# Seven block products instead of eight in the second feed-forward product of a top-k attention and ELU kernel

## The chip, the core and the metric

The kernel runs on one core of one Trainium2 chip. The metric is device time in microseconds. Before the change the median of three runs was 1619.19 us (1617.57 to 1620.54).

The engines are named as the profile names them: PE is the matrix engine (PEld its weight loads), DVE the vector engine, ACT the scalar engine, POOL the GpSimd engine, SP the engine that issues most transfers. SBUF is the on-chip memory, PSUM the memory that PE writes its products to; a bank of it holds 512 float32 values for each of 128 partitions.

## The reference

Inputs are q, k and v of 8 batches, 8 heads, 576 rows and 64 columns, a first weight matrix of 512 x 2048 and a second of 2048 x 512. Attention keeps the 32 highest scores of a row. Its result, 4608 tokens of 512 values, passes through a feed-forward layer with an ELU.

```python
scores = scale * np.matmul(q, k.transpose(0, 1, 3, 2))
kth = np.partition(scores, -top_k, axis=-1)[..., -top_k:-top_k + 1]
scores = np.where(scores >= kth, scores, -1000000000.0)
attn = np.exp(scores - np.max(scores, axis=-1, keepdims=True))
attn = attn / (np.sum(attn, axis=-1, keepdims=True) + 1e-09)
x = np.matmul(attn, v)            # heads side by side: 4608 x 512
h = x @ w_in                      # 4608 x 2048
g = np.where(h > 0.0, h, np.exp(np.minimum(h, 0.0)) - 1.0)
out = g @ w_out                   # 4608 x 512
```

Everything on PE is float32. One matmul of the source leaves two records of each kind in the trace, two weight loads and two matmuls.

## The kernel before

**Steps.** Attention is cut into 144 steps, 18 a batch. A step is one tile of 128 query rows with one pair of heads, or for the 64 rows that are left over in each batch one step for two pairs of heads. The main loop (line 711) writes, for step n, the instructions of several steps into the engines' queues, in an order fixed by hand (`manual_schedule`): the score products of step n + 2 on PE and their copy to SBUF on ACT (`scores`, lines 332 and 340), the search for the 32 highest of step n on DVE (`select`: 8 MAX8 and 6 MATCH_REPLACE8, lines 374 to 386), the masks of step n - 1 on ACT (`mask`, lines 406 and 407), its normalisation on POOL (`distance`, line 416, and `normalise`, lines 426 to 433), and for step n - 2 the transposes on PE and their copy on ACT (`turn`, lines 452 and 453). Once a group of tiles is turned, `attend` (line 479) multiplies it with v, and `finish` copies the result into `xT` (line 506). Each engine works through its own queue in order.

**Blocks.** The feed-forward layer works on blocks of one or two tiles of 128 tokens. The first two batches make five blocks of one tile (numbers 0 to 4) and two of two tiles; each later pair of batches makes four blocks of two tiles and one of one. That is 14 blocks of two tiles and 8 of one. When a block's attention is done, `ffn_pieces` adds its work to the list `ffn`, in pieces. A hidden piece (`hidden`) computes 128 of the 2048 hidden values for all tokens of the block: 4 matmuls whose moving operand has 256 columns for two tiles or 128 for one; then come the two halves of the ELU on ACT (lines 564 to 573) and their sum, the gate, on POOL (line 524) or DVE (line 526), which `close_gates` writes later. The result lies turned in `blk.gT`, as two halves of 8 chunks. A second-product piece (`project`) is a quarter of one tile's sum: 4 of 16 matmuls of 512 columns into one bank. The fourth piece of a tile copies the bank out (line 591) and stores it from SP's queue (line 594).

**Placing the pieces.** `feed` is called four times a step: after the first part of the search, after `mask(prev, 0)` and its part, after `turn` and `mask(prev, 1)` and their part, and after `normalise`. `normalise` so stands between the third and the fourth feed. A hidden piece of a two-tile block costs 1.85 units there, a second-product piece 3.55 (`PROJECT`). From the times at which blocks become ready, in steps, and from the work ahead of them (`due`), `feed` takes a pace in units a step and takes pieces from the list when half a piece's cost has come together.

**Buffers that the change touches.** `etpool` (2), `xpool` for `xT` of one-tile blocks (3), `opool` for the result (1), and the pools that `hook` opens once the weights have been decoded and the loading buffers are given up: `late["f"]` (two `n` buffers of 128 x 512), `late["g"]` (two halves of `gT`), `late["x"]` (two `xT`), `late["in"]`. `ps_f` has two banks for hidden and second products together.

Of the kernel before, what the change touches and what calls it, by code (L numbers as in the profile page):

```python
# [9 lines left out]
ALU = mybir.AluOpType  # L10
FP32 = mybir.dt.float32
# [9 lines left out]
HIDDEN = {1: 1.1, 2: 1.85}  # L21
PROJECT = 3.55
# [60 lines left out]
def kernel(  # L83
# [9 lines left out]
    nc = tc.nc  # L93
    P = nc.NUM_PARTITIONS
    B, H, S, D = q.shape
    dm, dff = moe_w_in.shape[0], moe_w_in.shape[1] // 2
# [5 lines left out]
    NC = dm // P  # L102
    NF = dff // P
    NG = NF // 2
    T = 2 * P
    KEYS, QUERIES = R, R + S
    Q = 32
# [5 lines left out]
    def pool(name, bufs, **kw):  # L113
        return ctx.enter_context(tc.tile_pool(name=name, bufs=bufs, **kw))
# [2 lines left out]
    kvpool = pool("kv", 5)  # L117
    scpool = pool("sc", 5)
    wkpool = pool("wk", 1)
    etpool = pool("et", 2)  # L120
    small = pool("small", 4)
    xpool = pool("x", 3)
    opool = pool("o", 1)
    ps_sc = pool("ps_sc", 1, space=PSUM)
    ps_t = pool("ps_t", 2, space=PSUM)
    ps_f = pool("ps_f", 2, space=PSUM)
    wide = [ps_sc.tile([P, 2, JP], FP32, tag=f"s{i}", name="scps") for i in range(2)]
    late = {}
    raws = ExitStack()
    early = raws.enter_context(tc.tile_pool(name="early", bufs=1))  # L130
    earlyf = raws.enter_context(tc.tile_pool(name="earlyf", bufs=2))
    ldpool = raws.enter_context(tc.tile_pool(name="ld", bufs=2))
# [7 lines left out]
    w_out = const.tile([P, NF, dm], FP32, tag="w_out", name="w_out")  # L140
# [59 lines left out]
    def hook():  # L200

        if not decode:
            return
        decode.pop(0)()
        if not decode:
            raws.close()
            late["f"] = ctx.enter_context(tc.tile_pool(name="f", bufs=2))
            late["g"] = ctx.enter_context(tc.tile_pool(name="g", bufs=2))
            late["x"] = ctx.enter_context(tc.tile_pool(name="xt", bufs=2))
            late["in"] = ctx.enter_context(tc.tile_pool(name="in", bufs=2))  # L210

    def decode_piece(i):
        if i + 3 < 2 * NF:
# [285 lines left out]

    def finish(blk, parts, at, cols, src):  # L500
        if blk.xT is None:
            if blk.slots == 1:
                blk.xT = xpool.tile([P, NC, P], FP32, tag="xT", name="xT")
            else:
                blk.xT = late["x"].tile([P, NC, T], FP32, tag="xT", name="xT")
        nc.scalar.copy(blk.xT[:, at, cols], src)
        blk.left -= parts
        if blk.left == 0:
            ffn.extend(ffn_pieces(blk))

    gates = []
    place = [0]

    def close_gates(keep=0, upto=None):

        while gates:
            put, group, dst, n, apart = gates[0]
            if put > place[0] - keep if upto is None else group > upto:  # L520
                return
            gates.pop(0)
            if apart:
                nc.gpsimd.tensor_tensor(dst, n, dst, ALU.add)  # L524
                continue
            nc.vector.scalar_tensor_tensor(
                out=dst, in0=n, scalar=-1.0, in1=dst, op0=ALU.add, op1=ALU.add
            )

    def ffn_pieces(blk):  # L530
        n_tok = blk.slots * P
        bank = dm // n_tok
        unit = max(2, bank)

        def hidden(f):
            if f == 0 and blk.number == 0:
                g = early.tile([P, NF, P], FP32, tag="g", name="gT")
                blk.gT = [g[:, 0:NG], g[:, NG:NF]]
            elif f % NG == 0 and blk.number > 0:
                g = late["g"].tile([P, NG, T], FP32, tag="g", name="gT")  # L540
                blk.gT.append(g[:])
            if f % unit == 0:
                if len(gates) > 1:
                    close_gates(upto=gates[0][1])
                if blk.number == 0:
                    n = earlyf.tile([P, 4 * P], FP32, tag="n", name="n")
                else:
                    n = late["f"].tile([P, 2 * T], FP32, tag="n", name="n")
                blk.n = n[:, 0 : unit * n_tok].rearrange("p (f t) -> p f t", f=unit)
            if f % bank == 0:  # L550
                ps = ps_f.tile([P, dm], FP32, tag="f", name="hps")
                blk.h = ps[:, 0 : bank * n_tok].rearrange("p (f t) -> p f t", f=bank)
            for i in range(NC):
                nc.tensor.matmul(  # L554
                    blk.h[:, f % bank, :],
                    w_in[:, i, f * P : (f + 1) * P],
                    blk.xT[:, i, 0:n_tok],
                    start=(i == 0),
                    stop=(i == NC - 1),
                )  # L560
            g, end = blk.gT[f // NG], f % NG + 1
            if end % bank == 0:
                n0 = f % unit + 1 - bank
                nc.scalar.activation(
                    blk.n[:, n0 : n0 + bank, :], blk.h, AF.Relu, scale=-1.0
                )
                nc.scalar.activation(g[:, end - bank : end, 0:n_tok], blk.h, AF.Relu)
            if end % unit == 0:
                nc.scalar.activation(blk.n, blk.n, AF.Exp, scale=-1.0)
                dst = g[:, end - unit : end, 0:n_tok]  # L570
                apart = place[0] > 4 * (tight + 3) and blk is not blocks[-1]
                if apart:
                    nc.scalar.activation(blk.n, blk.n, AF.Copy, bias=-1.0)  # L573
                gates.append((place[0], (blk.number, f + 1 - unit), dst, blk.n, apart))

        def project(s, part):
            close_gates(upto=(blk.number, (part + 1) * NF // 4 - 1))
            if part == 0:
                blk.o = ps_f.tile([P, dm], FP32, tag="f", name="ops")
            step = NF // 4  # L580
            for f in range(part * step, (part + 1) * step):
                nc.tensor.matmul(  # L582
                    blk.o[:],
                    blk.gT[f // NG][:, f % NG, s * P : (s + 1) * P],
                    w_out[:, f, :],
                    start=(f == 0),
                    stop=(f == NF - 1),
                )
            if part == 3:
                o = opool.tile([P, dm], FP32, tag="osb", name="osb")  # L590
                nc.scalar.copy(o[:], blk.o[:])
                for t in blk.tiles[s]:
                    p0 = t.cols.start - s * P
                    nc.sync.dma_start(out[t.rows, :], o[p0 : p0 + t.ql, :])

        part = HIDDEN[blk.slots]
        behind = 2 * NF if blk.number else 0
        return [
            (part, max(behind, NC * (f // 4 + 1)), lambda f=f: hidden(f))
            for f in range(NF)  # L600
        ] + [
            (PROJECT, max(behind, NF + (part + 1) * NF // 4),
             lambda s=s, part=part: project(s, part))
            for s in range(blk.slots)
            for part in range(4)
        ]

    ffn = []
    steps, first, due = [], {}, []
    blocks, tight = [], 2 * NHP  # L610
    for b in range(B):
        if b % 2 == 0:
# [5 lines left out]
            for part in division:  # L618
                blk = Block(len(blocks), len(part))
# [4 lines left out]
        for qt in range(J + 1):  # L624
# [8 lines left out]
            t = Tile(b, qt, rows, blk, slice(c0, c0 + n))  # L633
# [6 lines left out]
        for qts in order:  # L640
# [3 lines left out]
            for qt in qts:  # L644
                n = len(steps)
                tiles[qt].block.ready = n + 1.0 if n <= tight else n + 2.5
    NS = len(steps)
    total = 0.0
    for blk in sorted(blocks, key=lambda x: x.ready):
        due.append((blk.ready, total))  # L650
        total += NF * HIDDEN[blk.slots] + 4 * blk.slots * PROJECT

    todo = {}

# [3 lines left out]
    for b in range(1, B):  # L658
        f = first[b]
# [10 lines left out]
    def feed(n, share):  # L670

        place[0] += 1
        close_gates(2 if n < tight - 1 or n > tight + 1 else 6)
        fed["at"] = max(fed["at"], n)
        ahead = [(w - fed["sum"]) / (x - fed["at"]) for x, w in due if x > fed["at"]]
        if ahead:
            fed["over"] += max(0.0, share * min(ahead))
        fed["at"] += share
        while ffn and decoded[0] >= ffn[0][1] and 0.5 * ffn[0][0] <= fed["over"]:
            cost, _, piece = ffn.pop(0)  # L680
            fed["over"] -= cost
            fed["sum"] += cost
            piece()
# [118 lines left out]
```

## Time and profile before

| what | value |
|---|---|
| median of the runs | 1619.19 us |
| the profiled execution, its time | 1617.99 us |
| its span from first to last instruction | 1616.2 us |
| mean granted clock of PE | 0.974 |
| L554, hidden product: 2816 records | busy 541.8 us |
| L582, second product: 1152 records of 512 columns | busy 525.2 us |
| L386, MAX8 on DVE: 816 records | busy 654.2 us |
| L433, normalise on POOL: 288 records | busy 214.1 us |
| idle time of PE's transposes (L452) behind POOL's L433 | 32.9 us |

A row of a group reads: line, engine, operation, what is written and read, shapes, count, then busy time and mean duration in ns, then the idle time of the engine just before them and what ended it. A row of a stretch reads: the stretch, its length and PE's busy time, then PEld, DVE, ACT and POOL with counts, then the granted clock, the share of DMA and GB/s. A row of the waits names who waited for whom, the total, how often, and the longest. A row of the chain of waits, in order of time, has start, length and what ran; so has a row of the timeline, with the idle time before it in brackets. Busy time of PE is modelled and hides short gaps; the granted clock was below 1 only in the first 320 us.

### The profile page before, as it was taken

The page shows a single profiled execution, that of the slowest core. Times are in us where ns is not written, and L with a number is a line of the kernel's source. Part 1 is how long each engine was busy: PE and PEld are TensorE (multiplying, and loading weights), DVE is VectorE, ACT ScalarE, POOL GpSimd, SP SyncE. Part 2 cuts the span into 40 slices and gives each one's busy share as a digit, 9 for nine tenths or more (in the row PEclk, how much of TensorE's full clock was granted, in tenths as well). Part 3 has the DMA queues.
Part 4 walks back from the last instruction along what each step waited for, and adds up shares of the span by engine and source line. Part 5 has one row for each costly group of instructions (what it writes and reads, how often), then busy time and mean ns, then how long its engine had stood idle before and what let it go on. Part 6 is the DMA issues. An engine that isn't in the chain of part 4 may idle for free.

```text
span 1616.2 us, 25917 instructions
## 1 busy us (share of the span) xinstructions
PE 1572.3 (97%) x8660; PEld 1049.6 (65%) x8660; DVE 1451.6 (90%) x2981; ACT 1189.1 (74%) x2400; POOL 693.5 (43%) x1410
## 2 busy tenths in 40 slices
PE   5889999999999999999999999999999999999999
PEld 3565777666675757567475757577566666666764
DVE  6988999999999999999999599999999879999500
ACT  6988787778686868578686868777767776767831
POOL 3775444345353534345353444444434443533500
PEclk8579999999999999999999999999999999999999
DMA  7441220012100211002100121002200101000000
GB/s 220 157 136 27 51 41 23 8 22 45 43 1 14 43 33 28 14 16 50 38 8 7 23 51 37 8 8 44 52 15 7 22 16 36 1 14 7 1 13 14
DMA packets 188037, 56.21 MB, mean 35 GB/s; under 512 B 178176, under 2 KB 179200, under 8 KB 187904
## 3 DMA queue, kind: packets, MB, share of 16 engines
q1 hardware_dynamic: 186704, 54.26, 14.2%
q8 instruction: 69, 1.13, 0.3%
q14 instruction: 64, 0.52, 0.1%
q10 hardware_dynamic: 1200, 0.30, 0.1%
HBM read 45.09 MB, written 9.44 MB: 34 GB/s over the span
## 4 chain that ended last, share of the span: by engine, by line
PE 85%; ACT 6%; DVE 4%; POOL 2%; issue 1%; DMA 1%; SPq 0%; ACTq 0%; POOLq 0%
PE ops L582 30%; PE hps L554 28%; PE avps L479 9%; PE scps L332 9%; PE eps L452 7%; ACT sc L407 1%; DVE wk L379 1%; ACT et L453 1%; DVE m L386 1%; PE scps L452 1%; ACT sc L406 1%; DVE wk L355 1%; DVE m L361 1%; POOL sc L433 0%; ACT sc L340 0%
## 5 line engine op out<-in xcount | busy, mean ns | idle before, releaser
L386 DVE MAX8 m<-wk 128x8 f32<-128x576 f32 x816 | 654.2, 940 | 0.0
L554 PE MATMUL hps<-xT,w_in 128*128 128x256 f32 (+1 forms) x2816 | 541.8, 347 | 0.0
L582 PE MATMUL ops<-w_out,gT 128*128 128x512 f32 x1152 | 525.2, 601 | 0.0
L554 PEld LDWEIGHTS hps<-xT,w_in 128*128 128x128 f32 x2816 | 454.4, 193 | 68.9 <-issue 25.1
L379 DVE MATCH_REPLACE8 wk<-m,wk 128x576 f32<-128x576 f32 x544 | 452.2, 936 | 0.0
L582 PEld LDWEIGHTS ops<-w_out,gT 128*128 128x128 f32 x1152 | 210.3, 191 | 239.4 <-issue 235.0
L426 POOL TENSOR_SCALAR dene<-den 128x2 f32<-128x2 f32 x144 | 32.6, 226 | 655.4 <-ACT sc L407 654.9
L340 ACT ACTIVATE sc<-scps 128x576 f32<-128x576 f32 x288 | 171.6, 645 | 106.2 <-PE scps L332 106.2
L407 ACT ACTIVATE sc<-sc,den 128x576 f32<-128x576 f32 x288 | 224.0, 778 | 34.9 <-POOL den L416 18.8
L406 ACT ACTIVATE sc<-sc,m 128x576 f32<-128x576 f32 x288 | 226.3, 786 | 6.2 <-DVE m L386 6.2
L332 PE MATMUL scps<-kqT 64*128 64x288 f32 (+1 forms) x1280 | 213.6, 445 | 15.6 <-ACT kqT L308 9.3
L379 DVE MATCH_REPLACE8 wk<-m,sc 128x576 f32<-128x576 f32 x272 | 225.3, 930 | 0.0
L374 DVE MAX8 m<-sc 128x8 f32<-128x576 f32 x272 | 216.6, 932 | 5.5 <-ACT sc L340 5.5
L433 POOL TENSOR_SCALAR sc<-sc,rec 128x576 f32<-128x576 f32 x288 | 214.1, 754 | 14.9 <-POOL rec L431 0.2
L524 POOL TENSOR_TENSOR gT<-n,gT 128x512 f32<-128x512 f32 x131 | 167.3, 1277 | 78.3 <-ACT n L573 78.3
L453 ACT COPY et<-eps 128x512 f32<-128x512 f32 x288 | 153.8, 583 | 53.2 <-PE eps L452 53.0
L479 PE MATMUL avps<-et,vT 128*64 128x256 f32 (+2 forms) x2080 | 186.1, 326 | 3.0 <-ACT et L453 3.0
L332 PEld LDWEIGHTS scps<-kqT 64*128 64x128 f32 (+1 forms) x1280 | 113.5, 183 | 110.9 <-issue 53.6
L452 PEld LDWEIGHTS eps<-ident,sc 128*128 128x128 f32 x1152 | 136.3, 143 | 57.1 <-issue 30.3
L452 PE MATMUL eps<-ident,sc 128*128 128x128 f32 x1152 | 155.9, 278 | 13.2 <-POOL sc L433 12.9
L479 PEld LDWEIGHTS avps<-et,vT 128*64 128x64 f32 x2080 | 118.9, 141 | 74.4 <-issue 30.0
L379 DVE MATCH_VALUE_LOAD wk<-m,wk 128x8 f32 x544 | 146.9, 270 | 0.0
(53 smaller groups left out, 1171.5 us busy)
## 6 DMA issues: line engine op xcount, KB each, us to landing
raw<-in_moe_w_in_dram SPq DMA_DIRECT2D x16, 512.0 KB, 6.0
vT<-in_v_dram SPq DMA_DIRECT2D x64, 128.0 KB, 2.4
raw<-in_moe_w_out_dram SPq DMA_DIRECT2D x16, 512.0 KB, 3.9
out_dram<-osb SPq DMA_DIRECT2D x32, 256.0 KB, 2.0
kin<-in_k_dram SPq DMA_DIRECT2D x112, 72.0 KB, 2.4
qin<-in_q_dram SPq DMA_DIRECT2D x112, 72.0 KB, 2.4
kin<-in_k_dram SPq DMA_DIRECT2D x8, 128.0 KB, 4.5
vT<-in_v_dram SPq DMA_DIRECT2D x64, 16.0 KB, 2.1
```

The lines of the kernel that those rows point to most:

```text
L332: nc.tensor.matmul(wide[i][rows, half, 0:HS], kq[part, q0 : q0 + u.t.ql], kq[part, k0 : k0 + HS], start=True, stop=True,)
L340: nc.scalar.activation(u.sc[:, i, :].rearrange("p (a s) -> p a s", a=2), wide[i][:, :, 0:HS], AF.Copy, scale=scale,)
L374: nc.vector.max(found[i], cur[i])
L379: nc.vector.match_replace(wk[i], found[i], cur[i], TAKEN)
L386: nc.vector.max(found[i], cur[i])
L406: nc.scalar.activation(sc, sc, AF.Prelu, scale=-1.0, bias=low, alpha=1.0 / STEEP)
L407: nc.scalar.activation(sc, sc, AF.Exp, scale=-STEEP, bias=gap, accum_out=u.den[:, i : i + 1])
L433: nc.gpsimd.tensor_scalar(u.sc[:, i, :], u.sc[:, i, :], rec[:, i : i + 1], 1.0, ALU.mult, ALU.mult)
L452: nc.tensor.transpose(ps[:, c * P : (c + 1) * P], sc[:, c0 : c0 + P], ident[:])
L479: nc.tensor.matmul(ps[i * D : (i + 1) * D, cols], vt[:, 2 * J + i if c == J else i * J + c, :], w, start=(c == 0), stop=(c == J),)
L554: nc.tensor.matmul(blk.h[:, f % bank, :], w_in[:, i, f * P : (f + 1) * P], blk.xT[:, i, 0:n_tok], start=(i == 0), stop=(i == NC - 1),)
L582: nc.tensor.matmul(blk.o[:], blk.gT[f // NG][:, f % NG, s * P : (s + 1) * P], w_out[:, f, :], start=(f == 0), stop=(f == NF - 1),)
```

## The change

For two-tile blocks the second product is computed as a 2 x 2 product of blocks: the two tiles by the two halves of the 2048 hidden values (a11, a12 for the first tile, a21, a22 for the second; `gT[half][:, :, tile]`), times the two halves of the rows and of the 512 columns of `w_out` (B11, B12, B21, B22). Strassen's scheme in Winograd's form takes seven products of such blocks. Each has 8 matmuls of 256 columns. The sums of the a blocks are made on POOL, in place in `gT` and in two `n` buffers (`blk.s`); the results are copied by ACT from half a bank each and added on POOL in the result buffers. The sums of weight blocks t1 = B12 - B11, t2 = B22 - t1, t4 = B21 - t2 are made once on POOL, four instructions each, one at each feed after step 12 (`weight_sums`), and B12 is turned into B12 - B22 in place after block 4 (`fold_last`). One-tile blocks after that compute their right half as a1 (B12 - B22) + (a1 + a2) B22.

To make room, `etpool` goes from 2 buffers to 1, `xpool` lies with the early buffers, so that later one-tile blocks share `late["x"]`, and `opool` has 2 buffers. The planner counts 7 pieces of 3.55 for a two-tile block instead of 8.

```diff
-    etpool = pool("et", 2)
+    etpool = pool("et", 1)
     small = pool("small", 4)
-    xpool = pool("x", 3)
-    opool = pool("o", 1)
+    opool = pool("o", 2)
...
+    xpool = raws.enter_context(tc.tile_pool(name="x", bufs=3))
...
+            sums = ctx.enter_context(tc.tile_pool(name="sums", bufs=1))
+            for name in ("t1", "t2", "t4"):
+                late[name] = sums.tile([P, NG, HD], FP32, tag=name, name=name)
...
+            late["p"] = ctx.enter_context(tc.tile_pool(name="p", bufs=2))
+            weight_sums()
...
-            if blk.slots == 1:
+            if not late:
                 blk.xT = xpool.tile([P, NC, P], FP32, tag="xT", name="xT")
...
+    def weight_sums():
+        t1, t2, t4 = late["t1"], late["t2"], late["t4"]
+        for a, b, c in ((t1, B12, B11), (t2, B22, t1), (t4, B21, t2)):
+            for f in range(0, NG, 2):
+                part = slice(f, f + 2)
+                folding.append(
+                    lambda a=a, b=b, c=c, part=part: nc.gpsimd.tensor_tensor(
+                        a[:, part, :], b[:, part, :], c[:, part, :], ALU.subtract
+                    )
+                )
+    def fold_last():
+        while folding:
+            folding.pop(0)()
+        for f in range(0, NG, 2):
+            part = slice(f, f + 2)
+            nc.gpsimd.tensor_tensor(
+                B12[:, part, :], B12[:, part, :], B22[:, part, :], ALU.subtract
+            )
+        folded[0] = True
...
+        def product(dst, a, w, first=True, last=True):
+            for f in range(NG):
+                nc.tensor.matmul(
+                    dst, a(f), w[:, f, :],
+                    start=(first and f == 0), stop=(last and f == NG - 1),
+                )
+        def sum_up(dst, a, b, op):
+            for n in range(2):
+                part = slice(n * NG // 2, (n + 1) * NG // 2)
+                nc.gpsimd.tensor_tensor(dst(part), a(part), b(part), op)
...
+            else:
+                a1, a2 = piece(0, 0), piece(1, 0)
+                if part == 0:
+                    close_gates(upto=(blk.number, NF))
+                    blk.o = bank_tile("ops")
+                    blk.s = sum_tiles()
+                    sum_up(blk.s, a1, a2, ALU.add)
+                a, w = ((a1, B11), (a2, B21), (a1, B12), (blk.s, B22))[part]
+                half = slice(part // 2 * HD, (part // 2 + 1) * HD)
+                product(blk.o[:, half], a, w, part % 2 == 0, part % 2 == 1)
...
+        def project_pair(part):
+            a11, a21 = piece(0, 0), piece(0, 1)
+            a12, a22 = piece(1, 0), piece(1, 1)
...
+            if part == 0:
+                close_gates(upto=(blk.number, NF))
+                blk.o = [
+                    opool.tile([P, dm], FP32, tag="osb", name="osb") for _ in range(2)
+                ]
+                blk.s = sum_tiles()
+                sum_up(blk.s, a21, a22, ALU.add)
+            if part % 2 == 0:
+                blk.ps = bank_tile("ops")
+            ps = blk.ps[:, right if part % 2 else left]
...
+            if part == 0:
+                product(ps, a11, B11)
+                nc.scalar.copy(top[0], ps)
+            elif part == 1:
+                sum_up(a21, a21, a11, ALU.subtract)
+                sum_up(a11, blk.s, a11, ALU.subtract)
+                product(ps, blk.s, late["t1"])
+                blk.p5 = temp("p5")
+                nc.scalar.copy(blk.p5[:], ps)
+            elif part == 2:
+                sum_up(blk.s, a12, a11, ALU.subtract)
+                product(ps, a11, late["t2"])
+                nc.scalar.copy(top[1], ps)
+                add(top[1], top[1], top[0])
+            elif part == 3:
+                product(ps, a12, B21)
+                p = temp("px")
+                nc.scalar.copy(p[:], ps)
+                add(top[0], top[0], p[:])
+            elif part == 4:
+                product(ps, a21, B12)
+                nc.scalar.copy(low[0], ps)
+                add(low[0], low[0], top[1])
+                add(low[1], low[0], blk.p5[:])
+                add(top[1], top[1], blk.p5[:])
+            elif part == 5:
+                product(ps, blk.s, B22)
+                p = temp("px")
+                nc.scalar.copy(p[:], ps)
+                add(top[1], top[1], p[:])
+                store(0, blk.o[0])
+            else:
+                product(ps, a22, late["t4"])
+                p = temp("px")
+                nc.scalar.copy(p[:], ps)
+                add(low[0], low[0], p[:])
+                store(1, blk.o[1])
...
-        total += NF * HIDDEN[blk.slots] + 4 * blk.slots * PROJECT
+        total += NF * HIDDEN[blk.slots] + (4 if blk.slots == 1 else 7) * PROJECT
...
+        if folding and n > tight + 4:
+            folding.pop(0)()
```

More of the change, by code (lines that the diff above doesn't have):

```diff
@@ L104 @@
     NG = NF // 2
+    HD = dm // 2
     T = 2 * P
@@ L512, with bank_tile @@
     place = [0]
+    def bank_tile(name):
+        return ps_f.tile([P, dm], FP32, tag="f", name=name)
+    B11, B12 = w_out[:, 0:NG, 0:HD], w_out[:, 0:NG, HD:dm]
+    B21, B22 = w_out[:, NG:NF, 0:HD], w_out[:, NG:NF, HD:dm]
+    folding = []
+    def weight_sums():
[17 more added lines that the diff above has]
+        folded[0] = True
+    folded = [False]
     def close_gates(keep=0, upto=None):
@@ L550, in hidden @@
             if f % bank == 0:
-                ps = ps_f.tile([P, dm], FP32, tag="f", name="hps")
+                ps = bank_tile("hps")
                 blk.h = ps[:, 0 : bank * n_tok].rearrange("p (f t) -> p f t", f=bank)
@@ L574, in hidden @@
                 gates.append((place[0], (blk.number, f + 1 - unit), dst, blk.n, apart))
[L576 to L579, printed above, removed]
-            step = NF // 4
[L581 to L588, printed above, removed]
+        def product(dst, a, w, first=True, last=True):
[4 more added lines that the diff above has]
+                )
@@ new lines, in sum_up, with piece, sum_tiles, view @@
+        def sum_up(dst, a, b, op):
+            for n in range(2):
+                part = slice(n * NG // 2, (n + 1) * NG // 2)
+                nc.gpsimd.tensor_tensor(dst(part), a(part), b(part), op)
+        def piece(half, s):
+            g = blk.gT[half]
+            return lambda f: g[:, f, s * P : (s + 1) * P]
+        def sum_tiles():
+            ts = [late["f"].tile([P, 4 * P], FP32, tag="n", name="sT") for _ in range(2)]
+            vs = [t[:].rearrange("p (f t) -> p f t", f=NG // 2) for t in ts]
+            def view(f):
+                if isinstance(f, slice):
+                    return vs[f.start // (NG // 2)]
+                return vs[f // (NG // 2)][:, f % (NG // 2), :]
+            return view
@@ new lines, in store, with project @@
+        def store(s, o):
+            for t in blk.tiles[s]:
+                p0 = t.cols.start - s * P
+                nc.sync.dma_start(out[t.rows, :], o[p0 : p0 + t.ql, :])
+        def project(part):
+            step = NF // 4
+            if not folded[0]:
+                close_gates(upto=(blk.number, (part + 1) * step - 1))
+                if part == 0:
+                    blk.o = bank_tile("ops")
+                for f in range(part * step, (part + 1) * step):
+                    nc.tensor.matmul(
+                        blk.o[:],
+                        blk.gT[f // NG][:, f % NG, 0:P],
+                        w_out[:, f, :],
+                        start=(f == 0),
+                        stop=(f == NF - 1),
+                    )
+            else:
+                a1, a2 = piece(0, 0), piece(1, 0)
+                if part == 0:
+                    close_gates(upto=(blk.number, NF))
+                    blk.o = bank_tile("ops")
+                    blk.s = sum_tiles()
[3 more added lines that the diff above has]
+                product(blk.o[:, half], a, w, part % 2 == 0, part % 2 == 1)
@@ L591, in project, with add @@
                 nc.scalar.copy(o[:], blk.o[:])
-                for t in blk.tiles[s]:
-                    p0 = t.cols.start - s * P
-                    nc.sync.dma_start(out[t.rows, :], o[p0 : p0 + t.ql, :])
+                store(0, o)
+                if blk.number == plain:
+                    fold_last()
+        def project_pair(part):
+            a11, a21 = piece(0, 0), piece(0, 1)
+            a12, a22 = piece(1, 0), piece(1, 1)
+            left, right = slice(0, HD), slice(HD, dm)
+            temp = lambda name: late["p"].tile([P, HD], FP32, tag=name, name=name)
+            def add(dst, a, b):
+                nc.gpsimd.tensor_tensor(dst, a, b, ALU.add)
+            if part == 0:
[8 more added lines that the diff above has]
+            ps = blk.ps[:, right if part % 2 else left]
+            top = [blk.o[0][:, left], blk.o[0][:, right]]
+            low = [blk.o[1][:, left], blk.o[1][:, right]]
+            if part == 0:
+                product(ps, a11, B11)
[34 more added lines that the diff above has]
+                store(1, blk.o[1])
@@ L596, in ffn_pieces @@
         part = HIDDEN[blk.slots]
         behind = 2 * NF if blk.number else 0
-        return [
+        pieces = [
             (part, max(behind, NC * (f // 4 + 1)), lambda f=f: hidden(f))
             for f in range(NF)
-        ] + [
+        ]
+        if blk.slots == 2:
+            return pieces + [
+                (PROJECT, behind, lambda part=part: project_pair(part))
+                for part in range(7)
+            ]
+        return pieces + [
             (PROJECT, max(behind, NF + (part + 1) * NF // 4),
-             lambda s=s, part=part: project(s, part))
-            for s in range(blk.slots)
+             lambda part=part: project(part))
@@ L647 @@
     NS = len(steps)
+    plain = [blk.number for blk in blocks if blk.slots == 2][0] - 1
     total = 0.0
```

## The prediction

> **What bounds the kernel now.** I read the page's engine totals first, then the chain that ended last, then the groups by shape, the table of stretches, the waits, and the timeline of single steps.
>
> ```profile
> PE 1572.3 (97%) x8660; PEld 1049.6 (65%) x8660; DVE 1451.6 (90%) x2981; ACT 1189.1 (74%) x2400; POOL 693.5 (43%) x1410
> ...
> PE 85%; ACT 6%; DVE 4%; POOL 2%; issue 1%; DMA 1%; SPq 0%; ACTq 0%; POOLq 0%
> ...
> 1040.00:1120.00 80.00, 80.00 (x451) 53.30 (x450) 80.00 (x167) 57.19 (x116) 32.56 (x70) 1.00 0.11 22
> ...
> DVE kqT L286 <- PE scps L332: 37.3, 4, 16.8
> ...
> 918.10 3.65 PE hps L554 x16
> ...
> 1294.81 3.65 PE hps L554 x16
> ...
> 1557.28 27.63 PE hps L554 x128
> ...
> 1584.90 27.48 PE ops L582 x64
> ```
>
> Two engines look full. From 1040 to 1120 us both PE and DVE are busy for all 80 us, at a granted clock of 1.00, so busy shares can't say which one leads. Rates can. The work repeats every 36 steps (two batches). The chain of waits shows the same hidden piece at 918.10 and at 1294.81, so PE takes 376.7 us a period. DVE starts one step at 446.26 and the next at 455.89 in the timeline, 9.63 us, and a pair of transposes (L286) adds 1.35 us, eight pairs a period: 36 x 9.63 + 8 x 1.35 = 357.5 us. So PE is slower by 19 us a period. DVE runs up to 22 us ahead (from the end of a step's score products to its first MAX8), loses that lead, and is then held: the 37.3 us that L286 waits for PE, in four places, two of 16.8 us. From about step 36 (400 us) on, PE sets the time. Before that DVE does: the lead stands at 20 to 24 us from step 16 to 36, and PE waits there.
>
> **The products.** The tail has the clean rates. 128 records of N=256 (hidden, L554) take 27.63 us, 0.2159 each; 64 of N=512 (second product, L582) take 27.48 us, 0.4294 each. A matmul of the source leaves two records. A two-tile block had 2 x 16 matmuls of N=512, 64 records, 27.48 us. It gets 7 x 8 matmuls of N=256, 112 records: 112 x 0.2159 = 24.18 us. Saved: 3.30 us. A piece that follows other PE work begins 0.2 us later (8 records take 3.63 us in the chain after other work, 3.44 us in a run), and there are seven pieces for eight: 0.2 more. That makes **3.5 us a block**. There are 14 such blocks. One is the tail; the first, whose second product runs at about 386 to 430 us, lies where DVE paces PE, and I give it nothing. 12 x 3.5 = 42.0 us.
>
> What about 48 more weight loads a block? One takes 193 ns (L554) and N=256 streams for 216 ns, so it fits under the matmul before it; the hidden product is exactly this shape and shows no holes. [...]
>
> **What is added on GpSimd.** For each two-tile block four sums in two halves (8 tensor-tensors of 128x512) and seven adds of 128x256.
>
> ```profile
> L524 POOL TENSOR_TENSOR gT<-n,gT 128x512 f32<-128x512 f32 x131 | 167.3, 1277 | 78.3 <-ACT n L573 78.3
> ...
> L431 POOL TENSOR_TENSOR rec<-rec,dene 128x2 f32<-128x2 f32 x144 | 28.4, 197 | 12.0
> ...
> L506 ACT COPY xT<-avps 128x256 f32<-128x256 f32 x56 | 20.9, 373 | 44.7 <-PE avps L479 44.6
> ...
> L591 ACT COPY osb<-ops 128x512 f32<-128x512 f32 x36 | 21.1, 587 | 93.7 <-PE ops L582 93.7
> ...
> POOL dene L426 <- ACT sc L407: 654.9, 138, 13.2
> ```
>
> The wide sums are L524's shape: 8 x 1.277 = 10.2 us. A 128x256 add lies between 0.197 (2 columns) and 1.277 us (512); on the line between them it is 0.74, and seven are 5.2 us. So 15.4 us a block, 216 us in all. POOL goes from 694 to about 910 of 1616 us, 56%: it has room, and 655 us of its idle time is spent waiting for the softmax. ACT's copies go from 2 x 0.587 to 7 x 0.373 us, 1.4 us more a block, 20 us at 74% load. Neither total is on the path.
>
> **The order is.** POOL is a queue. An add after a product waits for ACT's copy, that for PE, and behind it stands normalise (L426 to L433), which releases PE's next transposes (L452). I took this loop from the timeline of the second-product stretch.
>
> ```profile
> 412.02 3.60 PE L582 MATMUL ops<-w_out,gT 128*128 128x512 f32 x8
> ...
> 415.55 1.24 PE L332 MATMUL scps<-kqT 64*128 64x288 f32 x8
> ...
> 416.72 3.70 PE L582 MATMUL ops<-w_out,gT 128*128 128x512 f32 x8
> ...
> 420.26 1.04 PE L452 MATMUL eps<-ident,sc 128*128 128x128 f32 x8
> ...
> 414.63 0.22 POOL L426 TENSOR_SCALAR dene<-den 128x2 f32<-128x2 f32 x1 [7.49 <-ACT sc L407]
> ...
> 416.59 1.48 POOL L433 TENSOR_SCALAR sc<-sc,rec 128x576 f32<-128x576 f32 x2
> ```
>
> Normalise ends at 418.07, 7.0 us after the transposes began at 411.04; the next begin at 420.26. The slack is 2.2 us in this short step (9.2 us) and 4.5 us in a long one (11.5 us, with L479's 2.31 us). Pieces come at every second of the four feeds of a step: 6.9 units a step, 3.55 a piece. Where they fall on the first and third feed, mask(prev, 0) on ACT now stands behind the first product's copy (normalise ends at +8.9, not +7.0), and normalise behind the third feed's add (+10.0; +11.5 for part 4 with its three adds). A short step then stalls PE for 0.4 to 2 us, a long one hardly. On the second and fourth feed the copy comes after that mask and the adds after normalise: no stall. Sums cost some 0.5 us where part 0's gates and sum (5.1 us) or part 1's two sums (5.1 us) sit ahead of normalise. Product 1 waits for part 0's sum, product 2 for part 1's, each with a piece and a transpose or score run (1 to 4.6 us) in between. Bounds: 0 a block if all fall well; 3.5 steps x 1.9 = 6.7 us if every step is caught. I take the middle of the two placements, about **1 us a block, 12 us**.
>
> A further wait: odd parts write the other half of the bank that ACT copies from. No such wait is in the trace; it is 0 if only the half is guarded, and about 0.65 us if the bank is (copy 0.2 us after the product, 0.373, a release). In steps 1 us of transposes or scores hides it. [...] I take 0.65, the upper end.
>
> **The tail.** Nothing hides these waits there. Products 24.18; bank waits before parts 1, 3 and 5, 3 x 0.65 = 1.95; part 2 waits for part 1's second sum (after sum, difference, difference on POOL) some 0.4. That is 26.5 for 27.48. At the end copy 0.37 and add 0.74 and a release 0.1 stand for a copy of 0.59. Gain: 0.95 - 0.62 = 0.3 us. If neither wait is there, 2.7 us.
>
> **Costed at nothing.** The turned weights: 16 tensor-tensors of 1.28 us, 20 us, once, at steps 13 to 16 and near 345 us; the DVE lead of 15 to 24 us covers them, and without it up to 5 us. The first has to wait for block 1's hidden products, which are out by step 12. One et buffer: ACT's copy waits for transposes that stand after the attention products (20 records of L479) in PE's order anyway. Single blocks share the two-buffer xT: the wait is for a hidden product two blocks earlier, some 8 steps; without that cover, up to 27.6 us a block. Later single blocks run 32 matmuls of N=256 for 16 of N=512, 64 x 0.2159 = 13.8 for 13.7 us, and POOL adds 2.6 us. SP's stores come one add later, ahead of loads that are issued a batch early.
>
> **The sum.** 42.0 + 0.3 - 12 = 30.3 us; the span 1616.2 becomes 1585.9. The profiled execution took 1617.99 us, 1.8 outside its span; the median of the runs is 1.2 above it. So about **1588 us**. DVE doesn't stop this: PE's period is 376.7 - 4 x 3.5 = 362.7, and DVE's 357.5.
>
> **Rivals.**
> (a) No new wait to speak of, as the slack of 2.2 and 4.5 us and POOL's 44% of free time allow: 42.0 + 2.7 saved, 1616.2 - 44.7 + 3.0 = 1574.5 us. Against it: the loop's +10 us in a 9.2 us step. Chance 0.24.
> (b) The loop takes 2.5 us a block, with part 4's adds often in short steps: 42 - 30 = 12 saved, about 1607 us; 1598 to 1615 counts here. Chance 0.15.
> (c) Slower: POOL's queue paces PE. Each of the 3.5 steps of a block's second product ends 1.9 us late, from the three adds and the sums ahead of normalise: 6.7 us a block, 12 x (6.7 - 3.5) = 38 lost, about 1657 us. It decides from 1 us a step on (3.5 / 3.5). For it: slack of hidden steps is only 0.5 us already. Against it: long steps have 4.5 us, and half of the placements put normalise first. Chance 0.10 (from 1623).
> (d) DVE bounds: without its 43 us of idle time after 400 us its last step ends at 1476, normalise comes 15 us later, and one piece, hidden 27.6 and the tail's 31 follow: a floor near 1557 us, below every sum here. That two-tile blocks don't take the new way can be excluded: the number of tiles alone chooses it; with the waits of lines 582 and 591 unchanged the time would be 1619. Chance of no change 0.03.
>
> The forecast, 1578 to 1598, has 0.48. The range reaches to 1571 for (a), whose upper gains need the first block too, and to 1607 through half of (b): about 0.80. What a measurement here can tell from no change is 0.2%, 3 us. Faster 0.87, within 0.03, slower 0.10.
>
> **What would show it.** 16 records a piece in about 3.46 us, and 112 for 64 a block; if a record takes more than 0.23 us, the loads are exposed. L286's wait for PE nearly gone, the DVE lead falling by about 5 us a period instead of 19. New idle time of PE at L452 behind POOL's sc, in second-product steps, about 12 us; if it is over 40, (c) holds. In the tail three holes of about 0.65 us. I am wrong if PE holes appear where no add precedes normalise, or if POOL's 512-column sums take well over 1.28 us beside DVE.

## The result and the profile after

The changed kernel takes 1642.14 us (median of four runs, 1639.87 to 1643.31) against 1619.87 us for the kernel before on the same chip: ratio 1.0136, 95% interval 1.0117 to 1.0155. It is 22 us slower. The forecast was 1588 us, range 1571 to 1607; the case with slower had been given 0.10. The profiled execution took 1639.87 us, its span is 1638.1 us. Line numbers moved: L452 is now L458, L433 L439, L479 L485, L554 L592, and the products stand in L617.

The page after, its engine totals and the chain that ended last by engine:

```profile
PE 1550.6 (95%) x9428; PEld 1206.9 (74%) x9428; DVE 1453.6 (89%) x2981; ACT 1204.3 (74%) x2470; POOL 925.5 (56%) x1642
...
PE 66%; ACT 17%; POOL 10%; issue 3%; DVE 3%; DMA 1%; SPq 0%; POOLq 0%; ACTq 0%
```

PE's busy time fell by 22 us while the span grew by 22. The chain left PE: 66% of it for 85%, and ACT and POOL, 8% together before, hold 27%. POOL's total is 925 us, where 910 had been forecast. So the loads came out as costed, and the time is lost in waiting.

The waits after (who waited for whom, total us, times, longest):

```profile
DVE kqT L292 <- PE scps L338: 41.3, 4, 16.8
...
ACT sc L413 <- POOL den L422: 34.8, 37, 3.1
...
PEld ops L617 <- POOL sT L626: 30.3, 12, 4.1
...
PE ops L617 <- POOL sT L626: 26.5, 11, 3.7
```

The last two rows are new. PE's second product waits 26.5 us for `sT`, the sum a21 + a22 that part 0 queues on POOL (PEld's row is the same wait, seen at the weight load). ACT waits 34.8 us for the small subtraction `den` at the start of a step (18.8 before). DVE is still held by PE, 41.3 us for 37.3: PE is the slower engine, as before. Its period of 36 steps is 380.5 us (from the score products of step 86 to those of step 122, 376.7 before).

One block shows how it happens, in the timeline (start, length, engine, line, operation; in brackets the idle time before it):

```profile
1241.59 0.22 POOL L432 TENSOR_SCALAR dene<-den 128x2 f32<-128x2 f32 x1 [4.62 <-ACT sc L413]
...
1242.03 3.72 PE L617 MATMUL ops<-w_out,gT 128*128 128x256 f32 x16
...
1243.55 1.47 POOL L439 TENSOR_SCALAR sc<-sc,rec 128x576 f32<-128x576 f32 x2
...
1244.99 1.28 POOL L562 TENSOR_TENSOR gT<-n,gT 128x512 f32<-128x512 f32 x1
1245.59 1.04 PE L458 MATMUL eps<-ident,sc 128*128 128x128 f32 x8
1246.23 0.19 POOL L422 TENSOR_TENSOR den<-m,m 128x2 f32<-128x2 f32 x1
1246.38 1.26 POOL L562 TENSOR_TENSOR gT<-n,gT 128x512 f32<-128x512 f32 x1
...
1246.46 0.27 PE L458 MATMUL scps<-ident,sc 128*128 128x128 f32 x1
...
1247.61 2.50 POOL L626 TENSOR_TENSOR sT<-gT 128x512 f32<-128x512 f32 x2
...
1248.92 5.41 PE L617 MATMUL ops<-t,sT 128*128 128x256 f32 x16 [2.19 <-POOL sT L626]
...
1250.40 0.23 POOL L432 TENSOR_SCALAR dene<-den 128x2 f32<-128x2 f32 x1 [0.28 <-ACT sc L413]
...
1253.80 2.50 POOL L626 TENSOR_TENSOR gT<-gT 128x512 f32<-128x512 f32 x2
```

Part 0 starts on PE at 1242.03. Its sum can't start on POOL before normalise of the step before (1241.59 to 1245.0), the last two gates of the block and `den` are through: 1247.61. PE is done with part 0 and the transposes at 1246.7 and stands for 2.19 us. From 1241.6 to beyond 1256 POOL waits for another engine only once, for 0.28 us. 56% over the span is full in these 15 us.

The same row shows a second loss: part 1 takes 5.41 us for 16 records, which take 3.6 to 3.7 us elsewhere. Eight of them come 0.43 us apart, half the rate. The stretches of the page say why:

```profile
1200.00:1280.00 80.00, 77.81 (x430) 60.71 (x427) 74.03 (x154) 60.18 (x123) 49.07 (x87) 0.98 0.02 8
```

The granted clock, 1.00 in every stretch after 320 us before the change, is 0.98 here. Up to the kernel's end the trace has six stretches of 3.4 us at half clock after 300 us, each behind such a hole, and a stretch costs 1.7 us.

### The profile page after: what moved, and what is told of

Same layout as the page of the kernel before. It is cut to its first block, busy times and chain, and to the rows that moved or that the text cites. A ratio compares the mean times of both kernels' runs of the same rounds, so it can differ in the third digit from the quotient of the medians.

```text
span 1638.1 us, 27746 instructions
## 1 busy us (share of the span) xinstructions
PE 1550.6 (95%) x9428; PEld 1206.9 (74%) x9428; DVE 1453.6 (89%) x2981; ACT 1204.3 (74%) x2470; POOL 925.5 (56%) x1642
## 4 chain that ended last, share of the span: by engine, by line
PE 66%; ACT 17%; POOL 10%; issue 3%; DVE 3%; DMA 1%; SPq 0%; POOLq 0%; ACTq 0%
PE ops L617 21%; PE hps L592 19%; PE avps L485 8%; PE scps L338 8%; PE eps L458 5%; PE ops L658 3%; ACT et L459 3%; ACT sc L413 3%; POOL sc L439 3%; ACT sc L412 3%; POOL gT L562 2%; ACT n L611 2%; POOL rec L434 1%; ACT n L602 1%; ACT n L607 1%
## 5 line engine op out<-in xcount | busy, mean ns | idle before, releaser
L392 DVE MAX8 m<-wk 128x8 f32<-128x576 f32 x816 | 578.0, 753 | 0.7 <-POOL den L422 0.7
L592 PE MATMUL hps<-xT,w_in 128*128 128x256 f32 (+1 forms) x2816 | 541.7, 346 | 0.0
L592 PEld LDWEIGHTS hps<-xT,w_in 128*128 128x128 f32 x2816 | 454.3, 193 | 67.0 <-issue 23.1
L385 DVE MATCH_REPLACE8 wk<-m,wk 128x576 f32<-128x576 f32 x544 | 401.4, 748 | 0.0
L413 ACT ACTIVATE sc<-sc,den 128x576 f32<-128x576 f32 x288 | 223.5, 776 | 48.7 <-POOL den L422 34.8
L338 PE MATMUL scps<-kqT 64*128 64x288 f32 (+1 forms) x1280 | 220.1, 446 | 15.5 <-ACT kqT L314 8.4
L439 POOL TENSOR_SCALAR sc<-sc,rec 128x576 f32<-128x576 f32 x288 | 213.2, 751 | 14.9
L380 DVE MAX8 m<-sc 128x8 f32<-128x576 f32 x272 | 191.8, 749 | 11.2 <-ACT sc L346 11.2
L385 DVE MATCH_REPLACE8 wk<-m,sc 128x576 f32<-128x576 f32 x272 | 200.6, 748 | 0.0
L485 PE MATMUL avps<-et,vT 128*64 128x256 f32 (+2 forms) x2080 | 186.3, 326 | 2.6 <-ACT et L459 2.5
L617 PE MATMUL ops<-w_out,gT 128*128 128x256 f32 x816 | 186.8, 383 | 0.5 <-ACT osb L716 0.5
L458 PE MATMUL eps<-ident,sc 128*128 128x128 f32 x1152 | 158.4, 279 | 22.4 <-POOL sc L439 21.8
L617 PEld LDWEIGHTS ops<-w_out,gT 128*128 128x128 f32 x816 | 151.5, 190 | 29.8 <-issue 8.0
L485 PEld LDWEIGHTS avps<-et,vT 128*64 128x64 f32 x2080 | 119.5, 141 | 72.6 <-issue 24.9
L458 PEld LDWEIGHTS eps<-ident,sc 128*128 128x128 f32 x1152 | 136.3, 144 | 45.1 <-POOL sc L439 30.4
L602 ACT ACTIVATE n<-hps 128x512 f32<-128x512 f32 x144 | 84.5, 587 | 66.6 <-PE hps L592 63.3
```

The source lines that it names most:

```text
L338: nc.tensor.matmul(wide[i][rows, half, 0:HS], kq[part, q0 : q0 + u.t.ql], kq[part, k0 : k0 + HS], start=True, stop=True,)
L385: nc.vector.match_replace(wk[i], found[i], cur[i], TAKEN)
L392: nc.vector.max(found[i], cur[i])
L413: nc.scalar.activation(sc, sc, AF.Exp, scale=-STEEP, bias=gap, accum_out=u.den[:, i : i + 1])
L439: nc.gpsimd.tensor_scalar(u.sc[:, i, :], u.sc[:, i, :], rec[:, i : i + 1], 1.0, ALU.mult, ALU.mult)
L458: nc.tensor.transpose(ps[:, c * P : (c + 1) * P], sc[:, c0 : c0 + P], ident[:])
```

## The experiments

Theory A: PE waits for a sum on POOL that stands behind normalise and the gates. Rival B: POOL's queue holds PE through normalise and the transposes wherever the sums stand. Ratios are to the kernel before on the same chip; medians of the kernel before were 1618.4 to 1620.4 us. Differences in us are between medians, in part of different chips; taken from the ratios they differ by up to 2 us. All variants are edits of the changed kernel unless said otherwise.

**Part 1 freed from the sum.**

```diff
-                product(ps, blk.s, late["t1"])
+                product(ps, a22, late["t1"])
```

> Part 1's matmuls read a22 where the scheme reads the sum a21 + a22, so that PE no longer waits for that sum; the sum is still made and read by part 5. Theory A (PE waits at part 1 for a sum that stands behind normalise and the last gates in POOL's queue: 29.6 us of holes before part 1 and five half-clock stretches of 1.7 us after them, 38 us in all): about 1604 us, no half clock after 300 us. Rival B (POOL's queue paces PE through normalise and the transposes anyway, so that the wait only moves to the next transposes): 1632 to 1645 us. Rival C (matmuls of 256 columns are dearer than in the hidden product): 1642 us, unchanged.

Measured: 1629.71 us, ratio 1.0071 (1.0056 to 1.0086). That is 12 us, not 38, and outside the ranges of all three theories; five half-clock stretches stay. What PE's L617 waited for in it (us of PE and PEld together, times), and the block at 950 us in the timeline:

```profile
  POOL gT L626: 39.7, 22
```

```profile
951.11 2.38 PE L485 MATMUL avps<-et,vT 128*64 128x256 f32 x20
957.64 4.61 PE L617 MATMUL ops<-t,gT 128*128 128x256 f32 x13 [4.15 <-POOL gT L626]
```

The wait for `sT` is gone and the wait for `gT`, part 1's own sums for part 2, has grown from 11.6 to 39.7 us. A in the narrow form, one wait at one place, is wrong, and so is B: PE's transposes wait 22.3 us for POOL's `sc`, for 21.8 in the changed kernel. What PE waits for is POOL's whole row of sums, and a freed place only shows the next one.

**No sums at all.** Parts 1, 2 and 5 of a two-tile block read a22, a11 and a12; all eight L626 instructions of the block go.

```diff
-                sum_up(blk.s, a21, a22, ALU.add)
...
-                sum_up(a21, a21, a11, ALU.subtract)
-                sum_up(a11, blk.s, a11, ALU.subtract)
...
-                sum_up(blk.s, a12, a11, ALU.subtract)
```

> Two-tile blocks leave out all four sums of token blocks on POOL (8 instructions of 1.28 us a block) and multiply a22, a11 and a12 as they are; copies, adds and matmul counts stay. Theory A: the holes before part 1 (38 us with the half clock) and part 2 (8.6 us) go: about 1596 us. Rival B: POOL's load is what matters, so this falls to 1585 us or below while the kernel that only frees part 1 stays above 1630. The ideal of the prediction without any new wait was 1575 us.

Measured: 1597.00 us, ratio 0.9871 (0.9856 to 0.9886), no half clock, as A had it. The sums cost the change 45 us, 3.2 us a block, and without them it would have been faster than before. The forecast of 1588 us isn't reached even so, and the 1575 us without any new wait are 22 us away.

**a12 x B21 moved to second place.**

```diff
-            elif part == 1:
+            elif part == 1:
+                product(ps, a12, B21)
+                blk.p2 = temp("px")
+                nc.scalar.copy(blk.p2[:], ps)
+            elif part == 2:
                 sum_up(a21, a21, a11, ALU.subtract)
```

> The same arithmetic; the product a12 x B21, which needs no sum, moves from fourth to second place, and its add to where the fourth piece was. The sum of part 0 gets one more piece (3.5 us) and at least 1 us of transposes or scores. Theory A: the holes of 2.0 to 3.9 us close and with them the half-clock stretches: 1600 to 1608 us, faster than the 1619.9 us of before. Rival B: unchanged within 8 us, 1634 to 1650.

Measured: 1622.14 us (10 runs), ratio 1.0024 (1.0015 to 1.0034). 20 us come back, half of what A asked for, and the time lies outside both ranges. Three sums are still queued within two pieces, and four half-clock stretches after 300 us stay. Their holes of 2.0 us are no waits for a sum any more: PE's wait for ACT's copy of part 4 (L725) has grown from 1.7 to 11.0 us. One of them in the timeline:

```profile
502.51 2.51 POOL L626 TENSOR_TENSOR sT<-gT 128x512 f32<-128x512 f32 x2
...
505.79 0.73 POOL L690 TENSOR_TENSOR osb<-osb,px 128x256 f32<-128x256 f32 x1
...
506.47 0.19 POOL L422 TENSOR_TENSOR den<-m,m 128x2 f32<-128x2 f32 x1
506.70 0.78 ACT L413 ACTIVATE sc<-sc,den 128x576 f32<-128x576 f32 x1 [3.48 <-POOL den L422]
...
507.47 0.35 ACT L725 COPY osb<-ops 128x256 f32<-128x256 f32 x1
...
507.97 2.63 PE L617 MATMUL ops<-w_out,sT 128*128 128x256 f32 x6 [2.00 <-ACT osb L725]
```

POOL's sum and adds stand ahead of `den`, ACT's mask waits for `den`, the copy of the product stands behind the mask, and PE waits for the copy before it writes the other half of the bank. So POOL's queue reaches PE by a second way, which neither A nor B names.

**Something to do in the hole.** Five matmuls whose result is overwritten, ahead of part 1, except in three blocks that had no such hole.

```diff
+                if blk.number not in (10, 15, 21):
+                    for f in range(5):
+                        nc.tensor.matmul(ps, a12(f), B21[:, f, :], start=True, stop=True)
                 product(ps, blk.s, late["t1"])
```

> Five more matmuls (10 records of 256 columns, 2.16 us) stand ahead of part 1 in those blocks that showed a hole there; their result is overwritten. PE is busy in the hole but can't end sooner for it. If the half clock comes from PE standing idle for 2.3 us or more: no half-clock stretch after 300 us, 5 x 1.7 = 8.5 us saved, some 1.5 us added where the hole was shorter than the filler: about 1635 us. If the half clock has another cause: 1642 us or more, with the half-clock stretches still there.

Measured: 1631.57 us, ratio 1.0082 (1.0067 to 1.0097): 10.6 us faster by more work (8.7 by the ratios). The same stretch as above, in this kernel:

```profile
1200.00:1280.00 80.00, 78.53 (x443) 61.95 (x442) 74.33 (x154) 60.33 (x126) 46.84 (x79) 1.00 0.01 4
```

The granted clock is 1.00 again, and none of the six stretches is left; 6 x 1.7 = 10.2 us is what they cost. So the half clock of these stretches came from PE standing idle.

**Sums spread, one with each piece.** Order a11 B11, a12 B21, a22 t4, then the products with sums. The pool `p` has one buffer of each name instead of two, as in all variants that build on this one.

```diff
+            elif part == 1:
+                sum_up(a21, a21, a11, ALU.subtract)
+                product(ps, a12, B21)
...
+            elif part == 2:
+                sum_up(a11, blk.s, a11, ALU.subtract)
+                product(ps, a22, late["t4"])
...
+            elif part == 3:
+                product(ps, blk.s, late["t1"])
...
+            elif part == 4:
+                sum_up(blk.s, a12, a11, ALU.subtract)
+                product(ps, a11, late["t2"])
...
+            elif part == 5:
+                product(ps, a21, B12)
...
+            else:
+                product(ps, blk.s, B22)
```

> The same arithmetic in the order a11 B11, a12 B21, a22 t4, then the four products that need sums; at most one sum of 2.5 us is queued on POOL with each piece, where the change queues three of them within two pieces, right behind the last gates. Theory A' (POOL is full for some 15 us between the last hidden piece and the third product, and a wait that is freed at one place comes back at the next, as it did when part 1 alone was freed): the holes ahead of products go, 1597 to 1606 us, close to the 1597 us of the kernel without any sum, and no half clock. Rival B' (what costs is that normalise and the mask's gap stand behind the sums anywhere in POOL's queue): no better than the reordered kernel, 1616 to 1624 us.

Measured: 1601.84 us, ratio 0.9889 (0.9873 to 0.9906). With all sums in place it comes within 5 us of the kernel without any, and their periods (step 86 to 122) are the same, 370.2 us. That settles A' against B': the load is the same, only its place in the queue and the order of the products differ. A' had no half clock at all, which isn't so: the profiled execution, the slowest of the four at 1606.44 us, has 3.4 us of it at 328 us and 6.8 us at 1393 us, both behind holes ahead of score products. No product waits for a sum any more. The same part of its timeline:

```profile
1226.71 2.52 POOL L626 TENSOR_TENSOR sT<-gT 128x512 f32<-128x512 f32 x2
1226.74 3.72 PE L617 MATMUL ops<-w_out,gT 128*128 128x256 f32 x16 [0.92 <-ACT osb L706]
...
1232.91 2.51 POOL L626 TENSOR_TENSOR gT<-gT 128x512 f32<-128x512 f32 x2
1233.88 3.72 PE L617 MATMUL ops<-t,gT 128*128 128x256 f32 x16
...
1235.54 2.52 POOL L626 TENSOR_TENSOR gT<-sT,gT 128x512 f32<-128x512 f32 x2
...
1238.42 3.62 PE L617 MATMUL ops<-t,sT 128*128 128x256 f32 x16
```

The sum ends 9 us before its product now, and that product runs at the full rate. What is left here is a wait for ACT's copy, 0.92 us: the bank's guard.

**Adds after normalise.**

```diff
-                nc.gpsimd.tensor_tensor(dst, a, b, ALU.add)
+                later.append(lambda: nc.gpsimd.tensor_tensor(dst, a, b, ALU.add))
...
             normalise(prev)
+        flush()
```

> The order of products of the spread kernel; the adds of results and the stores are written after normalise of the same step instead of right after their product. If an add that waits for PE and ACT holds normalise and so PE's transposes (the stall that the prediction priced at some 12 us): 5 to 12 us below the spread kernel. If the adds hold nobody, since POOL waits for the mask there anyway: within 3 us of it.

Measured: 1606.17 us, ratio 0.9918 (0.9904 to 0.9933), 4 us above spread, where 3 were allowed for adds that hold nobody. Writing them after normalise doesn't help, as it should if they held it; where the 4 us come from stays open.

**Adds cut to two columns**, in the changed kernel and in the fastest variant of the next paragraph.

```diff
-                nc.gpsimd.tensor_tensor(dst, a, b, ALU.add)
+                nc.gpsimd.tensor_tensor(dst[:, 0:2], a[:, 0:2], b[:, 0:2], ALU.add)
...
+                nc.scalar.copy(low[1], ps)
```

> The changed kernel with the seven adds of 256 columns of a two-tile block cut to 2 columns each (0.2 us for 0.73 us, 3.7 us less POOL time a block), and one copy of 0.37 us more on ACT in their place; the rest of each result stays unadded. The waits for PE and ACT that the adds bring into POOL's queue stay. Theory A' (the sums ahead of the third product cost the time, the adds do not): 1636 to 1643 us. Rival (the prediction's loop, where three adds of part 4 delay normalise by 2.2 us): 1625 to 1633 us.

> The fastest variant so far (products spread, gap on ACT) with the same cut of the adds to 2 columns. If the adds are free there: 1597 to 1601 us. If they still delay normalise: 5 us or more below its 1599.9.

Measured: 1641.02 us, ratio 1.0130 (1.0114 to 1.0145), and 1599.78 us, ratio 0.9876 (0.9858 to 0.9893). Each variant takes as long as its parent. In the fast variant that is clean: neither trace has half clock after 300 us, and the periods are 370.7 and 370.8 us. In the changed kernel it isn't. The holes ahead of part 1 are as long (26.7 us for 26.5), but eleven windows of 3.41 us lie at half clock behind them, for six. Without those, an estimate, the profiled execution would be some 5 us shorter than the changed kernel's (1641.3 - 18.8 for 1638.1 - 10.2). So the adds cost nothing where the sums are spread, and at most some 5 us in the changed kernel, where the sums cost 45.

**The gap on ACT.**

```diff
-            distance(prev)
...
-            mask(prev, 0)
+            mask(prev, 0, True)
```

(likewise for the other head)

> The spread kernel, with the gap between highest and lowest kept score made on ACT (two instructions of 0.31 us a step) instead of on POOL at the start of the step. ACT waited 47 us for that gap in the reordered kernel, 19 us before the change. If this wait passes on to ACT's copies and so to PE: 3 to 8 us below the spread kernel. If ACT's added 0.62 us a step weigh more: 0 to 5 us above it.

Measured: 1599.92 us, ratio 0.9879 (0.9864 to 0.9893); spread had 0.9889 (0.9873 to 0.9906). The intervals overlap. ACT's wait for `den` is gone by construction, and at most 2 us follow from it.

**The buffers alone, on the kernel before.**

```diff
-    etpool = pool("et", 2)
+    etpool = pool("et", 1)
-    opool = pool("o", 1)
+    opool = pool("o", 2)
...
-            if blk.slots == 1:
+            if not late:
```

> The kernel before, with the buffers of the change alone: one et buffer, two result buffers, xT of one-tile blocks with the early buffers and then shared, the room for the weight sums taken but not used. Every variant so far starts step 18 some 3 us later than before. If the buffers do that: 3 us above before, 1620 to 1623 us, with step 18 at 207 to 209 us. The prediction had costed them at nothing: 1618.4 us, step 18 at 205. Then the weight sums or the code would be behind the 3 us.

Measured: 1620.09 us, ratio 1.0004 (0.9994 to 1.0013). The buffers cost nothing. Step 18 starts at 206.7 us, for 205.2 before and 209.5 in the changed kernel. That the changed kernel reaches the score products of step 38 6.7 us later than before (410.7 for 404.0 us) is not from them. Variants reach it at 405 to 410 us; what makes this part vary stays open.

**A bank for each product**, on the variant with the gap on ACT.

```diff
-            if part % 2 == 0:
-                blk.ps = bank_tile("ops")
-            ps = blk.ps[:, right if part % 2 else left]
+            blk.ps = bank_tile("ops")
+            ps = blk.ps[:, left]
```

> The fastest variant (products spread, gap on ACT: 1599.9 us, ratio 0.9879) with a PSUM bank for each product instead of half a bank, so that no product waits for the copy of the one before it. Its trace shows three such waits of 0.5 us in the tail and four of 0.3 to 0.4 us before. If they are the bank's guard: none left, 2 to 3 us less, 1597 to 1598 us. If PE then only runs into the release of the bank of two products before: no change, 1599 to 1601 us.

Measured: 1595.27 us, ratio 0.9853 (0.9835 to 0.9872), the fastest kernel of this study. The chain at its end (start, length, what ran), and below it that of the changed kernel:

```profile
1539.79 24.82 PE hps L592 x115
1564.61 24.19 PE ops L617 x112
1588.80 0.02 issue
1588.82 0.38 ACT px L737
```

```profile
1608.69 1.89 issue
1610.59 0.38 ACT osb L706
1610.97 0.14 issue
1611.11 7.18 PE ops L617 x32
1618.29 0.02 issue
1618.31 0.38 ACT osb L716
...
1618.74 7.19 PE ops L617 x32
...
1625.99 0.38 ACT osb L725
1626.38 0.14 issue
1626.51 3.71 PE ops L617 x16
```

With half a bank each the chain passes through ACT's copy three times; with a bank each the seven products run as one piece.

## Why the prediction was wrong, step by step

**The bound: right.** PE led before, by 19 us a period, and still leads. The sign that went with the gain failed with it: DVE's wait for PE, which was to be nearly gone, is 41.3 us for 37.3.

**The products: right.** 112 records in 24.19 us in the last kernel's chain, 24.18 forecast. Over a period of the variant with the gap on ACT (step 86 to 122) the busy time of second-product records fell by 13.6 us (131.2 to 117.6), 14.0 forecast. Weight loads of 112 for 64 records stay hidden: a load of L617 takes 190 ns in the changed kernel (median), and the chain's records come 0.216 us apart, as those of the hidden product did before.

**The wait for sums: the step that failed.** The text reads "Sums cost some 0.5 us", and gave products 1 and 2 "a piece and a transpose or score run" to cover them. Measured: 45 us, 3.2 us a block, by leaving the sums out; 40 us of it by spreading them. The price counted how long a sum takes after its piece is issued, and not what is ahead of it in POOL's queue at that moment; it had the gates there as a delay of normalise, but neither gates nor normalise as a delay of the product. Normalise 3.4, two gates 2.5 and `den` 0.2 us were all in the trace of before; with the sum's first half, 1.2, they need 7.3 us from 1241.6, where the cover is one piece and a run of transposes, 4.7 us from 1242.0. Three sums within two pieces, 7.5 us, then meet the next normalise.

**The clock: not in the sum at all.** Idle holes of 2.19 to 3.67 us led to half clock for 3.4 us in six blocks: 10.6 us of the 45, measured by filling the hole. Three holes of 1.85 us and two of 2.18 and 2.27 us brought none. The traces show a pattern: in all 13 of them the clock changes only on a fixed grid of 3.413 us, and half clock goes with how long PE has no record, of products or transposes, within one window of the grid. Two windows of the changed kernel, each with the next (stretch, PE's busy time, granted clock):

```profile
1245.72:1249.14 3.42, 1.23 (x11) 1.00 0.00 0
1249.14:1252.55 3.41, 3.41 (x9) 0.50 0.02 5
866.84:870.26 3.42, 1.68 (x8) 1.00 0.00 0
870.26:873.67 3.41, 3.41 (x20) 1.00 0.02 5
```

The hole of 2.19 us lies in one window; of the one of 2.18 us, 1.74 us lie in the second window, the rest in the first. Of the windows at full clock after 200 us, in all traces, each of the 33 with 1.86 us or more without a record is followed by one at half clock, and none with up to 1.74 us; of the six between, five are. In the traces of before and after alone it is all eight with 2.19 to 2.94 us, and none with up to 1.85. So somewhat over half a window without a record was enough here.

**The adds: wrong in mechanism.** The loop from the first product's copy through adds to normalise was the one that the prediction watched, and rival (c) made it the slow case. Its sign came in near the price: the time that PE's transposes wait for POOL's `sc`, before and after the change (PE's own row, without PEld's):

```profile
PE eps L452 <- POOL sc L433: 12.9, 7, 3.8
```

```profile
PE eps L458 <- POOL sc L439: 21.8, 12, 5.1
```

That is 8.9 us more, with 12 forecast and over 40 for (c). But it is 19.6 us without any sums and 19.6 with the adds cut, so neither makes most of it. Moving the adds doesn't help (1606.17), and cutting them is worth nothing with the sums spread and at most some 5 us in the changed kernel. Rival (c) named the right queue and sign with the wrong instructions in it: of "the three adds and the sums ahead of normalise" it was the sums that counted, and not through normalise but at the products and, as the reordered kernel shows, through `den` and ACT's copies.

**The bank: right in size, too narrow in place.** The tail's waits came as forecast (0.65 us each; the chain shows 0.5 to 0.6 from the end of one product to the start of the next), and its 31.2 us from the first product to the end were forecast as 31.0. In steps "1 us of transposes or scores hides it" holds only while ACT is on time: spread shows 0.92 us. Of the two prices, 0 for a guard by half and 0.65 for one by bank, the second was the right choice: products wait for the copy of the other half of their bank, 11.0 us at L725 in the reordered kernel. A bank for each product, in whose trace L617 waits for no copy, gave 4.7 us by the medians, with 2 to 3 expected; the two intervals overlap a little.

**Costed at nothing: right for the buffers** (1620.09 us). The turning of the weights wasn't tried by itself.

**What stays open.** The sums explain 45 of the 54 us between the forecast and the result (the prediction's terms add to 1588.9, not 1588). With the sums spread and a bank for each product PE still gains 6.5 us a period instead of 14 (370.2 for 376.7). In the variant with the gap on ACT, which has nearly the same period, 3.0 us of the rest are longer times from record to record in the score products, and some 4 us are transposes that start late. That PE's shorter steps now run up against the loop of masks, copies and normalise is argued from that, not shown.

## What to carry to other kernels

A queue's load over the whole span says little for work that comes in bursts: take the stretch in which the new work falls due, list everything that stands ahead of it on that engine, and compare that sum with the time until its first reader. When one scheme offers several orders, put first the products that need nothing new, and issue helper work at the rate at which its engine is free. And where a wait is freed and little time comes back, look for the next wait of the same queue before the theory is dropped.

## What was not expected of the hardware

A PE that was otherwise busy lost its clock for a short hole: 2.19 us without a record, and the next eight records came 0.43 us apart instead of 0.216. Whether a hole did that went with where it fell on the grid of 3.413 us: holes of 2.00 us within one window brought half clock in the reordered kernel, one of 2.27 us across two windows brought none in the changed one. Useless matmuls in the hole made the kernel 10.6 us faster.
